# Attention plus two expert layers: value products four head pairs behind the scores, expert 0 released a pair later, and a third PSUM buffer for its first products

## The chip, the cores and the metric

The kernel runs on one core of one Trainium2 chip. The metric is the time of one execution on the device, in microseconds (us). Before the change three executions took 942.99, 941.4 and 942.53 us; the median is 942.53 us. The profile is of a further execution.

The core has five instruction queues that run side by side: TensorE (PE, matrix products into PSUM), VectorE (DVE), ScalarE (ACT), GpSimd (POOL) and SyncE (SP), which here only issues DMAs. Each takes its instructions in the order in which they stand in its queue, so an instruction that waits holds up all that stand behind it.

## The reference

```python
scores = scale * q @ k.T                      # (4, 8, 576, 576), head width 64
scores = where(0 <= rel < 128, scores + alibi, -1e9)
attn   = softmax(scores);  x = attn @ v       # -> x: 2304 tokens x 512
p   = domain_probs / sum(domain_probs)        # 4 experts, dense
out = sum_e p[:, e] * (relu(x @ w1[e]) @ w2[e])          # w1 512x1024, w2 1024x512
logits = out @ phi                            # 8 experts x 4 slots
slots  = softmax(logits, tokens).T @ out      # 32 x 512
slots  = relu(slots @ m1[e]) @ m2[e]          # per expert
return softmax(logits, slots) @ slots         # 2304 x 512
```

## The kernel before, in words

The 2304 tokens are 18 tiles of 128. To keep precision with 16-bit products, nearly every operand is split into a high and a low fp16 half, and a product is three matmuls (high by high, high by low, low by high).

**Attention** goes by head pairs: a tile has 8 heads, so 4 pairs, and the program has 72 of them, numbered 0 to 71 (tile i holds pairs 4i to 4i+3). One pass of the main loop (`for n in range(NS + LAG + 3)`) writes out, in this order:

- `qk` for pair n: the scores, 8 matmuls (12 or 10 where a tile holds the end of a sequence, 4 where it begins one), into one of two PSUM tiles tagged S0 and S1 (lines 336 to 341);
- `soft` for pair n: bias and row minimum on DVE (L353), the exponential on ACT (L358), the high half on ACT (L363), the low half on POOL (L364), and then a transpose of the 128 x 1024 result into `eT`. For tiles 0 and 1 the transposes are done by PE (L303), for the other 16 tiles by a DMA that SP issues (L299);
- the loads and transposes of q, k and v of the next tiles (lines 276 to 321), which use the same SP queue;
- some work of expert 0 from the list `pend`;
- `pv`: the value products of the pair m with `pvt(m) == n` (L381, 12 matmuls). `pvt(m)` is m + 1 for the first four pairs and m + LAG, with LAG = 3, for the rest.

When a tile's last pair has its value products, `xn` and `xn_c` normalise it, split it and transpose it into `xT` (lines 387 to 395 and L299 again).

**Expert 0** works on attention's output as it comes, so that PE has something to do while the chain of DVE, ACT, POOL and SP makes the next `eT`. Tiles are taken in groups: tiles 0 to 3 singly, then by twos. A group becomes available a number of passes after its last value product (`avail`). Its first-layer products are 8 pieces of 12 matmuls (`l1_piece`, L206; called L1.k below, 8 per group, numbered through), 128 columns wide for a single tile and 256 for two. Each piece fills a PSUM tile tagged L1, of which there are two, and is split by ACT (L220) and DVE (L221), which frees the tile. The second layer is 24 matmuls per tile (`l2_mm`, L234) into one of two PSUM tiles tagged L2, and is read by DVE (L242). The tag L2 also serves the PE transposes. A group's second layer is queued between the first-layer pieces of the next group (`queue_moe0`).

The program is recorded with the tile framework, which is asked to schedule it (`schedule_with_timeline_sim=True`): the order of the instructions in each queue is worked out when the kernel is built, with the program's order as priority. So work written later can stand earlier in a queue where its inputs and its buffer are free by then.

After attention come what is left of expert 0, then experts 1 to 3, most of them by seven products in place of eight (L585 and L660), then the slot layer with the loads of `m1` and `m2`.

Of the kernel before, what the change touches and what calls it, by code (L numbers as in the profile page):

```python
# [8 lines left out]
F32 = mybir.dt.float32  # L9
F16 = mybir.dt.float16  # L10
# [9 lines left out]
def kernel(  # L20
# [14 lines left out]
    P = 128  # L35
# [24 lines left out]
    ps = ctx.enter_context(tc.tile_pool(name="ps", bufs=2, space=bass.MemoryType.PSUM))  # L60
    ps2 = ctx.enter_context(tc.tile_pool(name="ps2", bufs=2, space=bass.MemoryType.PSUM))
# [4 lines left out]
    def nm(s):  # L66
        uid[0] += 1
        return f"{s}_{uid[0]}"

    def sl(shape, dt, name, pool=None):  # L70
        return (pool or slab).tile(shape, dt, tag="slab", name=nm(name))
# [101 lines left out]
    def w1_ap(e, fc, hl, kc):  # L173
        o = kc * 256 + (fc % 2) * P
        return W[e, fc // 2, 0][:, hl, o:o + P]
# [12 lines left out]
    def x_ap(t0, n, xa, kc):  # L188
        o = (t0 % TS) * P
        return xT[t0 // TS][:, xa, kc, o:o + n]  # L190
# [8 lines left out]
    hh = {}  # L199

    def l1_piece(e, t0, n, fc, key):
        pt = ps.tile([P, 512], F32, tag="L1", name=nm("l1"))[:, 0:n]
        first_mm = True
        for kc in range(KC):
            for wa, xa in ((0, 0), (0, 1), (1, 0)):
                nc.tensor.matmul(pt, lhsT=w1_ap(e, fc, wa, kc), rhs=x_ap(t0, n, xa, kc),  # L206
                                 start=first_mm, stop=(kc == KC - 1 and wa == 1))
                first_mm = False
        if e == 0:
            kk = (key, fc // 4)  # L210
            if kk not in hh:
                hh[kk] = sl([P, 4, 2, 256], F16, "h")
            ht = hh[kk][:, fc % 4, :, 0:n]
        else:
            kk = (key, fc // 2)
            if kk not in hh:
                hh[kk] = h3[h3n[0] % 2].rearrange("p (a b c) -> p a b c", a=2, b=2)
                h3n[0] += 1
            ht = hh[kk][:, fc % 2, :, 0:n]
        nc.scalar.activation(out=ht[:, 0], in_=pt, func=AF.Relu)  # L220
        nc.vector.scalar_tensor_tensor(out=ht[:, 1], in0=pt, scalar=0.0, in1=ht[:, 0],  # L221
                                       op0=ALU.max, op1=ALU.subtract)

    l2p = {}
    h3n = [0]

    def l2_mm(e, t, o, fcs, key, lo, hi):
# [18 lines left out]
    def moe_pieces(e, tl, fcs, init):  # L246
        key = nm("hk")
        n = len(tl) * P
        r = [(12 * n * 0.422, lambda fc=fc: l1_piece(e, tl[0], n, fc, key)) for fc in fcs]
        for j, t in enumerate(tl):  # L250
            nf = len(fcs)
            for lo in range(0, nf, 4):
                hi = min(lo + 4, nf)

                def f(t=t, j=j, lo=lo, hi=hi):
                    l2_mm(e, t, j * P, fcs, key, lo, hi)
                    if hi == nf:
                        l2_add(e, t, l2p.pop((key, t)), init)
                r.append((3 * (hi - lo) * 216, f))
        return r  # L260
# [5 lines left out]
    sums, nmx, es, eT, xps, xfs = {}, {}, {}, {}, {}, {}  # L266

    def at(shape, dt, tag, bufs=2):
        return ap_.tile(shape, dt, tag=tag, name=nm(tag), bufs=bufs)
# [22 lines left out]
    def sp_v_lo(i):  # L292
        a, t = raw["v", i], vvs[i]
        nc.vector.scalar_tensor_tensor(out=t[:, :, 1], in0=a, scalar=VS, in1=t[:, :, 0],
                                       op0=ALU.mult, op1=ALU.subtract)

    def trans(dst, src, nb, pe):
        if not pe:
            nc.sync.dma_start_transpose(out=dst, in_=src)  # L299
            return  # L300
        pt = ps2.tile([P, 8, P], F16, tag="L2", name=nm("tp"))
        for j in range(nb):
            nc.tensor.transpose(pt[:, j], src[:, j * P:(j + 1) * P], ident16)  # L303
        hb = nb // 2
        nc.vector.tensor_copy(dst[:, 0:hb], pt[:, 0:hb])
        nc.scalar.activation(out=dst[:, hb:nb], in_=pt[:, hb:nb], func=AF.Copy)
# [16 lines left out]
    def kbs(i):  # L323
        return [1] if i in first else [0, 1]
# [19 lines left out]
    def soft(i, hp, st):  # L344
        kb0 = kbs(i)[0]
        if hp == 0:
            sums[i] = at([P, H], F32, "sums")
            nmx[i] = at([P, H], F32, "nmx")
        c0, w = kb0 * P, (2 - kb0) * P
        et = at([P, 2, 2 * P], F32, "e", 3)  # L350
        for hl in range(2):
            h = 2 * hp + hl
            nc.vector.tensor_tensor_reduce(out=et[:, hl, c0:], in0=st[:, hl, c0:], in1=bias[:, h, c0:],  # L353
                                           op0=ALU.add, op1=ALU.min, scale=-0.125, scalar=3.0e38,
                                           accum_out=nmx[i][:, h:h + 1])
        for hl in range(2):
            h = 2 * hp + hl
            nc.scalar.activation(out=et[:, hl, c0:], in_=et[:, hl, c0:], func=AF.Exp, scale=-1.0,  # L358
                                 bias=nmx[i][:, h:h + 1], accum_out=sums[i][:, h:h + 1])
        e2 = at([P, 2, 2, 2 * P], F16, "e2", 3)  # L360
        if kb0:
            e2 = e2.rearrange("p a b c -> p (a b c)")[:, 0:4 * P].rearrange("p (a b c) -> p a b c", a=2, b=2)
        nc.scalar.activation(out=e2[:, :, 0], in_=et[:, :, c0:], func=AF.Copy)  # L363
        nc.gpsimd.tensor_tensor(out=e2[:, :, 1], in0=et[:, :, c0:], in1=e2[:, :, 0], op=ALU.subtract)  # L364
        nb = 4 * w // P
        eTt = at([P, 8, P], F16, "eT", 6)
        trans(eTt[:, 0:nb], e2.rearrange("p a b c -> p (a b c)"), nb, i < 2)
        eT[i, hp] = eTt

# [31 lines left out]

    ld(0)
    bias = at([P, H, 2 * P], BF16, "bias", 1)
    scr = at([P, 2 * P], F32, "scr", 1)
    make_identity(nc, ident16)
    build_bias(scr)
    build_small()
# [14 lines left out]
    swap_q(0)  # L422
    sp_v_hi(0)
    sp_v_lo(0)
    LAG = 3
    NS = NT * 4
    PE_T = 2

    def pvt(m):
        return m + (1 if m < 4 else LAG)  # L430

# [3 lines left out]
        groups0.append(list(range(b0, b0 + z)))  # L435
    avail = []
    for tl in groups0:
        avail.append((pvt(4 * tl[-1] + 3) + (3 if tl[-1] else 1), tl))
    pend = []
    late = []  # L440

# [12 lines left out]
    budget = 0.0  # L454
    for n in range(NS + LAG + 3):
        i, hp = divmod(n, 4)
# [6 lines left out]
        if n < NS:  # L463
            soft(i, hp, st)
# [26 lines left out]
        while avail and avail[0][0] <= n:  # L491
            tl = avail.pop(0)[1]
# [173 lines left out]
    while avail:  # L666
        tl = avail.pop(0)[1]
# [317 lines left out]
    for st in range(2):  # L985
        for hf in range(2):
            hps = ps.tile([P, 512], F32, tag="L1", name=nm("hp"))
            for kc in range(KC):
                for g in range(4):
                    e = 4 * st + g  # L990
# [14 lines left out]
        for g in range(4):  # L1005
            e = 4 * st + g
# [52 lines left out]
```

## Time and profile before

| what | before |
|---|---|
| median of three executions | 942.53 us |
| profiled execution: its time | 942.66 us |
| profiled execution: its span in the profile | 940.9 us |
| PE busy in the span | 877.4 us (93%) |
| DVE, ACT, POOL busy | 577.1, 372.6, 189.3 us |
| mean granted share of PE's clock | 0.983 |

The span is the stretch from the first to the last instruction that the profile shows; the execution's own time lies 1.76 us above it. In the rows below a window `A:B` is in us from the start of the span. `PEclk` is the share of TensorE's full clock of 2.4 GHz that was granted (1.00, or 0.50 at 1.2 GHz; in between it is a mean over the window). A row of the timeline gives start, length, engine, line, operation and tiles; in brackets stands how long the engine was idle just before and what ended it.

### The profile page before, as it was taken

How to read it: one execution, taken by the hardware profiler on the slowest of the kernel's cores; microseconds unless marked ns; L12 is line 12 of the kernel's file. 1: busy time of each engine (PE TensorE's matmuls, PEld its weight loads, DVE VectorE, ACT ScalarE, POOL GpSimd, SP SyncE). 2: the span in 40 equal slices, each digit the busy share in tenths (PEclk: the TensorE clock that was granted, in tenths of full speed). 3: DMA queues.
4: the chain of work that ended last, by engine and by line, in shares of the span. 5: the costliest groups of instructions: out<-in, count | busy, mean ns of one | idle time of the engine just before them, and what ended most of it. 6: DMA issues, size and time to landing. Idle time of an engine off the chain costs nothing.

```text
span 940.9 us, 16481 instructions
## 1 busy us (share of the span) xinstructions
PE 877.4 (93%) x6514; PEld 512.3 (54%) x6514; DVE 577.1 (61%) x1234; ACT 372.6 (40%) x920; POOL 189.3 (20%) x176
## 2 busy tenths in 40 slices
PE   3489988889999999999999999999999999999797
PEld 2366766667765655555555555555555445554432
DVE  9954655576549387657575766666666464456512
ACT  5786666677734243323132323232333202223412
POOL 7765455566420000000000000000000005310000
PEclk9799999999999999999999999999999999999799
DMA  9599999999850110100101010101001008974695
GB/s 261 113 188 183 176 187 154 192 181 186 140 130 28 47 45 3 43 23 22 45 1 45 1 46 1 45 13 33 23 23 46 1 1 326 209 204 139 236 387 222
DMA packets 222031, 102.37 MB, mean 109 GB/s; under 512 B 187217, under 2 KB 201585, under 8 KB 221953
## 3 DMA queue, kind: packets, MB, share of 16 engines
q1 hardware_dynamic: 212320, 78.14, 39.2%
q10 hardware_dynamic: 6800, 13.11, 4.0%
q0 software_dynamic: 2832, 10.07, 2.9%
q8 instruction: 51, 0.84, 0.4%
q14 instruction: 28, 0.22, 0.1%
HBM read 64.59 MB, written 4.72 MB: 74 GB/s over the span
## 4 chain that ended last, share of the span: by engine, by line
PE 76%; DMA 7%; issue 5%; ACT 4%; POOL 3%; DVE 3%; SPq 2%; POOLq 0%; ACTq 0%; DVEq 0%
PE l L660 22%; PE A L585 12%; PE l L206 11%; PE l L234 10%; PE C L585 6%; PE B L585 3%; ACT e L358 2%; PE hp L991 2%; DMA qT<-qs 2%; PE x L381 2%; PE so_ps L1009 2%; DMA m<-in_moe_w_dram 1%; PE s L341 1%; DMA eT<-e 1%; PE fp L1022 1%
## 5 line engine op out<-in xcount | busy, mean ns | idle before, releaser
L660 PE MATMUL l<-w,h 128*128 128x512 f16 x1080 | 252.8, 379 | 0.0
L244 DVE SCALAR_TENSOR_TENSOR acc<-l,pr,acc 128x512 f32<-128x512 f32 x216 | 161.4, 748 | 127.1 <-PE l L660 103.3
L585 PEld LDWEIGHTS <-w 128*128 128x128 f16 x1260 | 123.3, 98 | 94.0
L206 PE MATMUL l<-xT,w 128*128 128x256 f16 (+2 forms) x1344 | 160.5, 271 | 12.6 <-DVE h L221 8.1
L660 PEld LDWEIGHTS <-h 128*128 128x128 f16 x1080 | 105.7, 98 | 115.2
L234 PE MATMUL l<-w,h 128*128 128x512 f16 x648 | 153.1, 381 | 0.7 <-DVE acc L244 0.7
L206 PEld LDWEIGHTS <-w 128*128 128x128 f16 x1344 | 115.9, 99 | 46.2 <-issue 10.1
L609 ACT ACTIVATE ct<-A 128x384 f32<-128x384 f32 x90 | 43.5, 487 | 218.9 <-PE A L585 218.9
L754 POOL DMA_DIRECT2D m<-in_moe_w_dram x19 | 13.8, 725 | 510.1 <-DVE h L605 446.9
L234 PEld LDWEIGHTS <-h 128*128 128x128 f16 x648 | 61.9, 98 | 64.4 <-issue 2.6
L364 POOL TENSOR_TENSOR e<-e,e 128x512 f16<-128x512 f32 (+1 forms) x72 | 81.4, 1133 | 55.7 <-ACT e L363 33.7
L221 DVE SCALAR_TENSOR_TENSOR h<-l,h 128x256 f16<-128x256 f32 (+2 forms) x112 | 45.0, 409 | 62.5 <-ACT h L220 62.1
L220 ACT ACTIVATE h<-l 128x256 f16<-128x256 f32 (+2 forms) x112 | 40.2, 365 | 106.5 <-PE l L206 69.3
L358 ACT ACTIVATE e<-e,nmx 128x256 f32<-128x256 f32 (+1 forms) x144 | 69.9, 487 | 29.3 <-DVE nmx L353 29.1
L585 PE MATMUL C<-xs,w 128*128 128x384 f16 x360 | 71.2, 326 | 0.0
L585 PE MATMUL A<-xs,w 128*128 128x384 f16 x360 | 69.3, 326 | 0.0
L585 PE MATMUL A<-xT,w 128*128 128x384 f16 x360 | 67.6, 326 | 0.0
L353 DVE CUSTOM_DVE_ANT_0 e<-s,bias 128x256 f32<-128x256 f32 (+1 forms) x144 | 52.6, 403 | 19.4 <-PE s L341 15.8
L604 ACT ACTIVATE h<-ct 128x384 f16<-128x384 f32 x90 | 43.8, 515 | 46.5 <-PE l L660 25.1
L336 PE MATMUL s<-kT,qT 128*128 128x128 f16 x272 | 44.9, 228 | 9.3 <-DVE nmx L353 5.1
L381 PE MATMUL x<-vv,eT 128*128 128x64 f16 x816 | 39.3, 197 | 11.5 <-DMA eT<-e 7.3
L605 DVE SCALAR_TENSOR_TENSOR h<-ct,h 128x384 f16<-128x384 f32 x90 | 47.6, 550 | 2.3 <-ACT h L604 2.1
(181 smaller groups left out, 964.6 us busy)
## 6 DMA issues: line engine op xcount, KB each, us to landing
m<-in_moe_w_dram ACTq DMA_DIRECT2D x25, 512.0 KB, 5.5
stg<-in_moe_w_dram SPq DMA_DIRECT2D x20, 512.0 KB, 4.7
m<-in_moe_w_dram SPq DMA_DIRECT2D x20, 512.0 KB, 10.2
m<-in_moe_w_dram POOLq DMA_DIRECT2D x19, 512.0 KB, 11.6
stg<-in_moe_w_dram SPq DMA_DIRECT2D x24, 256.0 KB, 3.3
out_dram<-ots SPq DMA_DIRECT2D x18, 256.0 KB, 3.4
qr<-in_q_dram SPq DMA_DIRECT2D x16, 256.0 KB, 3.8
kr<-in_k_dram SPq DMA_DIRECT2D x16, 256.0 KB, 4.1
```

The source lines that it names most:

```text
L206: nc.tensor.matmul(pt, lhsT=w1_ap(e, fc, wa, kc), rhs=x_ap(t0, n, xa, kc), start=first_mm, stop=(kc == KC - 1 and wa == 1))
L221: nc.vector.scalar_tensor_tensor(out=ht[:, 1], in0=pt, scalar=0.0, in1=ht[:, 0], op0=ALU.max, op1=ALU.subtract)
L234: nc.tensor.matmul(pt, lhsT=ht[:, ha, o:o + P], rhs=w2_ap(e, fc, wa), start=(fc == fcs[0] and ha == 0 and wa == 0), stop=(fc == fcs[-1] an ...
L244: nc.vector.scalar_tensor_tensor(out=a, in0=pt, scalar=p, in1=a, op0=ALU.mult, op1=ALU.add)
L336: nc.tensor.matmul(o, lhsT=qT[i][:, 0, h], rhs=mv, start=True, stop=False)
L353: nc.vector.tensor_tensor_reduce(out=et[:, hl, c0:], in0=st[:, hl, c0:], in1=bias[:, h, c0:], op0=ALU.add, op1=ALU.min, scale=-0.125, scal ...
L358: nc.scalar.activation(out=et[:, hl, c0:], in_=et[:, hl, c0:], func=AF.Exp, scale=-1.0, bias=nmx[i][:, h:h + 1], accum_out=sums[i][:, h:h ...
L364: nc.gpsimd.tensor_tensor(out=e2[:, :, 1], in0=et[:, :, c0:], in1=e2[:, :, 0], op=ALU.subtract)
L381: nc.tensor.matmul(o, lhsT=t[:, (hl * 2 + ea) * nk + kb - kb0], rhs=vvs[i - 1 + kb][:, h, va], start=(kb == kb0 and ea == 0 and va == 0), ...
L585: nc.tensor.matmul(o, lhsT=wq_[:, blk, wa, kc], rhs=xf(xa, kc), start=(first and kc == 0 and wa == 0 and xa == 0), stop=(kc == 1 and wa == 1),
L605: nc.vector.scalar_tensor_tensor(out=o[:, 1], in0=src, scalar=0.0, in1=o[:, 0], op0=ALU.max, op1=ALU.subtract)
L660: nc.tensor.matmul(pt, lhsT=u["h"][:, z, ha, par, i * P:(i + 1) * P], rhs=w2_ap(e, 2 * qd + z, wa), start=(z == 0 and ha == 0 and wa == 0) ...
```

## The change

The value products trail the scores by four pairs (LAG = 4). The release of a group of expert 0 is counted from the value products, so it moves along; for groups that end at tile 2 or later it is one pair later still. Every third first-layer piece of expert 0 takes its PSUM tile from the tag L2 in place of L1. `eT` has seven buffers for six, and the scratch tile of the bias borrows the first of `e`'s three buffers, which makes the room.

```diff
     def l1_piece(e, t0, n, fc, key):
-        pt = ps.tile([P, 512], F32, tag="L1", name=nm("l1"))[:, 0:n]
+        l1n[0] += e == 0
+        pool, tg = (ps2, "L2") if e == 0 and l1n[0] % 3 == 0 else (ps, "L1")
+        pt = pool.tile([P, 512], F32, tag=tg, name=nm("l1"))[:, 0:n]
...
     l2p = {}
+    l1n = [0]
...
-        eTt = at([P, 8, P], F16, "eT", 6)
+        eTt = at([P, 8, P], F16, "eT", 7)
...
-    scr = at([P, 2 * P], F32, "scr", 1)
+    scr = at([P, 2, 2 * P], F32, "e", 3)[:, 0]
...
-    LAG = 3
+    LAG = 4
...
-        avail.append((pvt(4 * tl[-1] + 3) + (3 if tl[-1] else 1), tl))
+        avail.append((pvt(4 * tl[-1] + 3) + (4 if tl[-1] > 1 else 3 if tl[-1] else 1), tl))
```

The number of instructions on every engine stays the same; the schedule gives them another order up to the end of expert 0, and nearly the same one after it. Three places are shown. The changed kernel's line numbers are 3 higher from its second edit on (2 higher inside `l1_piece`), and the numbers in tile names are given anew.

SP's queue, where the DMA transposes of `eT` begin (pair 8). `qT` and `kT` are the transposed q and k of tiles 3 and 4, `qr`, `kr`, `vr` loads; `eT_703` and `eT_740` are pairs 8 and 9. Before:

```order
L299 DMA_TRANSPOSE qT_745<-qs_708 128x8x128
L299 DMA_TRANSPOSE kT_784<-ks_747 128x8x128
L276 DMA qr_875<-in_q_dram 128x8x64
L276 DMA kr_911<-in_k_dram 128x8x64
L276 DMA vr_1023<-in_v_dram 128x8x64
L299 DMA_TRANSPOSE eT_703<-e_117_700 128x8x128
L299 DMA_TRANSPOSE qT_913<-qs_877 128x8x128
L299 DMA_TRANSPOSE eT_740<-e_123_737 128x8x128
L299 DMA_TRANSPOSE kT_1025<-ks_915 128x8x128
```

Now, with `eT_690` and `eT_728` as pairs 8 and 9:

```order
L302 DMA_TRANSPOSE qT_733<-qs_695 128x8x128
L302 DMA_TRANSPOSE kT_772<-ks_735 128x8x128
L279 DMA qr_862<-in_q_dram 128x8x64
L279 DMA kr_899<-in_k_dram 128x8x64
L279 DMA vr_937<-in_v_dram 128x8x64
L302 DMA_TRANSPOSE qT_901<-qs_864 128x8x128
L302 DMA_TRANSPOSE kT_939<-ks_903 128x8x128
L302 DMA_TRANSPOSE eT_690<-e_116_687 128x8x128
L302 DMA_TRANSPOSE eT_728<-e_123_725 128x8x128
```

Both transposes of tile 4 now stand ahead of those of pairs 8 and 9.

PE's queue from the scores of pair 28 to the first product of tiles 4 and 5 (L1.32), one row for each step. Before, `s_1951`, `s_1989` and `s_2089` are the scores of pairs 28 to 30, `eT_1806` the value products of pair 25, `l_330_2116` a second layer, `l_318_2016` L1.32:

```order
L336 MATMUL s_1951<-kT_1600,qT_1810 128x128
...
L381 MATMUL x_1938<-vv_1347,eT_1806 128x64
...
L234 MATMUL l_330_2116<-w_312,h_1562 128x512
...
L336 MATMUL s_1989<-kT_1600,qT_1810 128x128
...
L336 MATMUL s_2089<-kT_1600,qT_1810 128x128
...
L206 MATMUL l_318_2016<-xT_445,w_206 128x256
```

Now, `s_1929`, `s_1977`, `s_2015`, `s_2054` and `s_2148` are pairs 28 to 32, `eT_1709`, `eT_1763` and `eT_1832` the value products of pairs 24 to 26, `l_329_2075` L1.32:

```order
L339 MATMUL s_1929<-kT_1572,qT_1767 128x128
...
L384 MATMUL x_1964<-vv_1260,eT_1709 128x64
...
L384 MATMUL x_1964<-vv_1260,eT_1763 128x64
...
L339 MATMUL s_1977<-kT_1572,qT_1767 128x128
...
L384 MATMUL x_1964<-vv_1260,eT_1832 128x64
...
L339 MATMUL s_2015<-kT_1572,qT_1767 128x128
...
L339 MATMUL s_2054<-kT_1572,qT_1767 128x128
...
L339 MATMUL s_2148<-kT_1836,qT_1998 128x128
...
L208 MATMUL l_329_2075<-xT_445,w_206 128x256
```

The second-layer products (19 matmuls in a row before) have left this stretch; they stand behind L1.35 now, and two more pairs' scores stand ahead of L1.32.

PE's queue around the value products of pair 42, one row for each step. Before, `s_2903` and `s_2959` are the scores of pairs 45 and 46, `eT_2763` is pair 42, `l_466_2931` is L1.48, the first product of tiles 8 and 9:

```order
L381 MATMUL x_2838<-vv_2359,eT_2703 128x64
...
L336 MATMUL s_2903<-kT_2545,qT_2707 128x128
...
L381 MATMUL x_2838<-vv_2359,eT_2763 128x64
...
L336 MATMUL s_2959<-kT_2545,qT_2707 128x128
...
L206 MATMUL l_466_2931<-xT_2168,w_206 128x256
```

Now, with `s_2917` and `s_2970` as pairs 46 and 47, `eT_2713` as pair 42 and `l_477_2991` as L1.48:

```order
L384 MATMUL x_2835<-vv_2289,eT_2668 128x64
...
L339 MATMUL s_2917<-kT_2488,qT_2672 128x128
...
L237 MATMUL l_442_2780<-w_394,h_2249 128x512
...
L384 MATMUL x_2835<-vv_2289,eT_2713 128x64
...
L339 MATMUL s_2970<-kT_2488,qT_2672 128x128
...
L208 MATMUL l_477_2991<-xT_2177,w_206 128x256
```

Pair 42's value products now stand behind the scores of pair 46 and 12 second-layer matmuls; L1.48 stands one pair later.

## Rows read from the trace of the kernel before

**Rows 1.** The page: busy time of each engine, share of the span, instructions.

```profile
PE 877.4 (93%) x6514; PEld 512.3 (54%) x6514; DVE 577.1 (61%) x1234; ACT 372.6 (40%) x920; POOL 189.3 (20%) x176
```

**Rows 2.** Windows: length; busy PE, PEld, DVE, ACT, POOL; PEclk; DMA share; GB/s.

```profile
45.00:65.00 20.00, 15.40 (x247) 12.75 (x244) 12.98 (x47) 16.07 (x50) 13.59 (x12) 1.00 0.97 174
65.00:114.00 49.00, 45.26 (x614) 33.89 (x612) 25.64 (x90) 31.43 (x95) 25.91 (x22) 0.97 1.14 192
114.00:124.00 10.00, 8.53 (x105) 6.06 (x102) 7.97 (x28) 8.20 (x26) 6.78 (x6) 1.00 0.95 136
124.00:157.00 33.00, 28.16 (x311) 20.67 (x310) 15.28 (x54) 20.38 (x62) 17.61 (x17) 1.00 1.05 183
157.00:245.00 88.00, 80.02 (x905) 60.09 (x904) 56.89 (x172) 62.90 (x180) 51.44 (x44) 0.96 1.04 177
245.00:275.00 30.00, 30.00 (x331) 21.78 (x328) 13.94 (x49) 15.99 (x47) 12.68 (x11) 1.00 0.63 107
275.00:800.00 525.00, 525.00 (x2862) 279.89 (x2861) 338.80 (x567) 150.00 (x310) 15.36 (x21) 1.00 0.13 42
```

**Rows 3.** What PE waited for from 45 to 275: us in total, times, longest.

```profile
PE l L206 <- DVE h L221: 8.1, 6, 2.4
PE x L381 <- DMA eT<-e: 7.3, 6, 2.4
PE l L206 <- DMA xT<-xs: 3.5, 2, 2.0
PE s L336 <- DVE nmx L353: 2.6, 1, 2.6
```

**Rows 4.** Timeline of PE at five of its waits.

```profile
93.94 0.83 PE L206 MATMUL l<-xT,w 128*128 128x128 f16 x12 [2.24 <-DVE h L221]
...
123.35 2.79 PE L206 MATMUL l<-xT,w 128*128 128x256 f16 x24 [1.47 <-DMA xT<-xs]
...
151.72 0.52 PE L381 MATMUL x<-vv,eT 128*128 128x64 f16 x12 [2.43 <-DMA eT<-e]
...
178.04 0.52 PE L381 MATMUL x<-vv,eT 128*128 128x64 f16 x12 [1.85 <-DMA eT<-e]
...
180.69 2.52 PE L206 MATMUL l<-xT,w 128*128 128x256 f16 x12 [2.02 <-DMA xT<-xs]
```

**Rows 5.** Windows around the three stretches at half clock, and one wait without.

```profile
91.00:95.00 4.00, 1.76 (x39) 1.49 (x35) 1.92 (x7) 1.50 (x6) 2.15 (x2) 1.00 1.02 197
95.00:100.00 5.00, 5.00 (x57) 3.95 (x55) 2.60 (x12) 3.60 (x12) 1.15 (x1) 0.66 0.97 195
138.00:142.00 4.00, 1.59 (x21) 1.38 (x19) 2.38 (x9) 2.72 (x8) 1.15 (x1) 1.00 1.01 209
177.00:181.00 4.00, 0.94 (x17) 0.75 (x18) 1.62 (x2) 2.05 (x4) 3.08 (x3) 1.00 1.00 200
181.00:185.00 4.00, 4.00 (x22) 2.63 (x21) 2.88 (x11) 2.53 (x9) 1.04 (x2) 0.58 1.21 228
...
198.00:202.00 4.00, 4.00 (x32) 2.77 (x30) 2.91 (x11) 3.97 (x14) 1.89 (x2) 0.57 0.90 175
```

**Rows 6.** The chain that ended last, from 244 to 262: start, us, what.

```profile
254.45 0.35 PE x L381 x12
...
255.25 0.35 PE x L381 x12
...
256.04 2.62 PE l L206 x24
```

**Rows 7.** SP's queue, line 299: ns min/median/max, first and last start.

```profile
L299 SPq DMA_TRANSPOSE eT<-e x64: 1205/1291/2581, 53.3 to 267.2; - x64
```

**Rows 8.** Timeline of SP where the transposes of eT begin.

```profile
55.34 1.25 SPq L299 DMA_TRANSPOSE qT<-qs  x1
...
58.08 1.51 SPq L299 DMA_TRANSPOSE kT<-ks  x1
```

**Rows 9.** Timeline of PE: the value products of pair 23.

```profile
113.44 0.51 PE L381 MATMUL x<-vv,eT 128*128 128x64 f16 x12
```

## The prediction, made before the changed kernel was run

> **What bounds the kernel now.** I read the page first: PE is busy for 93% of the span, no other engine for more than 61% [rows 1]. Then busy time by stretch, which shows where PE's idle time lies [rows 2]. From 245 to 800 PE is busy without a gap, so nothing there can be gained but by taking work out, and the change takes none out: every engine has as many instructions as before, and the order after expert 0 is nearly the same. Up to 45 the first loads and the first tiles rule, and the order there is the same as well. What is left is 45 to 245. In the five windows that cover it PE is idle for 4.60, 3.74, 1.47, 4.84 and 7.98 us, together 22.6 (length less busy PE) [rows 2]. The list of waits says for what: 8.1 us for DVE to empty a PSUM tile of the first layer, 7.3 for the DMA that brings `eT`, 3.5 for the DMA that brings `xT`, 2.6 for DVE to empty a score tile [rows 3]; the rest is the start. The timeline gives the single waits, none over 2.63 us [rows 3, 4].
>
> To that comes the clock. Three stretches ran at 1.2 GHz: the windows at 95, 181 and 198 have a granted clock of 0.66, 0.58 and 0.57 with PE busy throughout, which is 0.34 x 5 + 0.42 x 4 + 0.43 x 4 = 5.1 us lost. Before the first two PE had been busy for 1.76 and 0.94 of 4 us [rows 5]. So 22.6 + 5.1 = 27.7 us are the whole of what this change can give back, 2.9% of the time.
>
> The rest of PE's time up to the end of attention is work that stays. At full clock a pair's value products take 0.35 us and its scores 0.45 (255.25 less 254.45 less 0.35), two 256-column pieces of the first layer 2.62 [rows 6]. A piece of expert 0 that is not done during attention is done after it at the same cost, with PE busy. What counts is therefore only how much idle time and how much half clock there is in the new order; I go through it by the five stretches.
>
> **45 to 65 (pairs 8 to 16).** SP's queue has the transposes of tile 4's q and k ahead of that of pair 8. They took 1.25 and 1.51 us [rows 8], so pair 8's `eT` comes up to 2.8 us later, and POOL must make those halves first. The value products of pairs 8 to 10 stand close together on PE with little else between them, since the pieces L1.0 to L1.7 are all queued ahead. Bounds: no loss, if the low half of pair 8 is late anyway, and 2.8 us. I take two thirds of it: idle 4.6 + 1.8 = 6.4.
>
> **65 to 114.** 3.74 us of idle, all before first-layer products that waited for DVE; 2.24 of it at 93.94 [rows 2, 4]. With three PSUM tiles in rotation such a piece waits for the split three pieces back and not two; a 128-column piece is some 0.8 us [rows 4], so the third tile covers one such step and the later lag and release put other work there too. Bounds 0 and 3.74; I take 0.5. What is late next is PE's own work.
>
> **114 to 124 (pairs 27 to 32).** Here the order gets worse. The second layer that ran between the scores of pairs 28 and 29 has moved behind L1.35, since L1.32 and L1.35 take L2 tiles ahead of it. From the end of pair 23's value products, which open tiles 4 and 5, to L1.32 it took 123.35 - 113.95 = 9.4 us, and L1.32 waited 1.47 of them for `xT` [rows 4, 9]. That path (normalise, split, SP, DMA) is not shortened. PE now has between the two only the scores of five pairs and the value products of three: 5 x 0.45 + 3 x 0.35 = 3.3. Idle: 9.4 - 3.3 = 6.1, for 1.47 now. Bounds: 1.47, if the scores spread over the same time as now, and above by the pace of the chain: SP's seven transposes per tile at 1.29 us [rows 7] are 2.26 us a pair, five pairs 11.3, less 3.3, is 8.0. I take 6.1.
>
> **124 to 157 (pairs 33 to 43).** The wait of 2.4 us for DVE before a first-layer piece [rows 3] goes, that of 2.43 before pair 34's value products [rows 4] goes with the longer lag. But L1.40 again needs the last value products of its group, pair 31, and behind them stand only the scores of pairs 36 to 42, the first four of them half as long (4 x 0.22 + 3 x 0.45 = 2.2), and the value products of four pairs (1.4). By the same 9.4 us the idle time is 5.8, for 4.84 now. Bounds 2.4 (one wait as now), and by SP's pace 7 x 2.26 - 3.6 = 12.2.
>
> **157 to 245 (pairs 44 to 63).** The order is even here: with each pair come its scores, the value products of the pair four back and one or two pieces of expert 0. The waits of 1.85 (`eT`) and 2.02 (`xT`) at 178 to 181 [rows 4] go: pair 42's products stand a pair and 12 second-layer matmuls later, and L1.48 behind them. The wait for DVE of 2.63 [rows 3] came from a score tile and may stay in part. Bounds 0 and 7.98; I take 1.5.
>
> The other two edits cost nothing: `scr` is read by DVE before the first scores, long before its buffer is wanted again, and a seventh `eT` buffer holds the one pair more that is now under way.
>
> **The clock.** All three present stretches at half clock follow waits that I let go. In the new order PE is thinly busy in the two bare stretches (3.3 of 9.4 us and 3.6 of 9.4), about as thinly as before two of the present three, while after 138 to 142 with 1.59 of 4 us busy it did not fall [rows 5]. I take one stretch of 1.7 us for each of the two, 3.4 for 5.1. Bounds 0 and 8.5 (one in each of the five stretches).
>
> The Trainium skill speaks against the change here: "TensorE: Matmul & The Clock Gate", section "Part 1: The HAM clock gate", has the low clock as the state that an engine falls back to and activity as what lifts it. By that rule the thin stretch at 45 to 65 would cost a third fall, and the sum would be 1.7 us higher. The trace agrees in the three falls and not in the wait at 138.
>
> **The sum.** Idle 6.4 + 0.5 + 6.1 + 5.8 + 1.5 = 20.3 for 22.6, half clock 3.4 for 5.1: 4.0 us less. The profiled execution took 942.66 us, of which 940.9 are its span; 942.66 - 4.0 = 938.7. The median shown is 942.53, 0.13 below the profiled one; I let that stand and predict 938.7.
>
> **Rivals.**
>
> *The bare stretches are paced by the chain (slower).* A score tile is free for the pair after next only when DVE has read it, and DVE, ACT and POOL go on only as their buffers come free behind SP's transposes. If pairs 28 to 32 and 36 to 42 go at SP's 2.26 us a pair, the two stretches cost 8.0 + 12.2 and not 11.9, and the stretch before each gives a third fall of the clock: 938.7 + 8.3 + 1.7 = 948.7. It decides from 4 us more idle time than I put there, about 16 us in the two together. For it: `eT` transposes now start 213.9 us apart over 63 steps, 3.4 us a pair, and the new order starves this chain while PE does expert 0 in long blocks. Against it: the buffers let two or three pairs of scores run ahead, and the path to `xT` ends first. Chance 0.21.
>
> *The waits stay where the lag does not reach.* From 157 on only the waits for `eT` go (1.85 and what is like it), while those for `xT` and for DVE (2.02 + 2.63 = 4.65) stay in some form: 938.7 + 4.65 - 1.5 = 941.8. For it: the change does nothing to the path from value products to `xT`. A form of it is that the third PSUM tile does not help, as two of three pieces still share two tiles: 65 to 114 keeps 3.74 us and its fall of the clock, 938.7 + 3.2 + 1.7 = 943.6. Chance of both together 0.24; both are no change.
>
> *The bare stretches cost nothing.* If value products and scores spread so that PE idles there no longer than now (1.47 + 4.84 = 6.3 for 11.9) and the clock holds, 938.7 - 5.6 - 3.4 = 929.7. Chance 0.08.
>
> **How the numbers follow.** My forecast has 0.47, with a range of its own of 934 to 941. About 0.2% (1.9 us) is what a measurement of this kernel can tell from no change, since its three executions lie 1.6 us apart; the forecast and the last rival are faster by more, the second lies within, the first is slower. Some of the forecast's spread falls within 0.2%, some of the middle rival's outside it on either side: 0.54 faster, 0.24 the same, 0.22 slower. For 8 in 10 the range leaves out the last rival and the outer half of the first: 931.5 to 947.
>
> **What would show it.** Right: from 65 to 114 and from 157 to 245 PE is idle for under 3 us in all, no wait for `eT` behind pair 40; an idle stretch of 5 to 7 us ends with L1.32 on `xT`, a second with L1.40; attention's last value products come 5 to 9 us earlier than now. Wrong: L1.32 starts later than about 125 us or L1.40 later than about 155 (the chain sets the pace), falls of the clock at more than two places, or waits of 2 us and more among pairs 44 to 63. If PE idles anywhere between 245 and 800, the order behind attention matters after all, and the sum lacks a term.

## The result, and the profile after

| what | before | after |
|---|---|---|
| median | 942.18 us (6 runs, 941.09 to 945.7) | 950.05 us (6 runs, 947.66 to 952.67) |
| ratio | | 1.0077, 95% interval 1.006 to 1.0093 |
| profiled execution: time, span | 942.66, 940.9 us | 947.66, 945.9 us |
| mean granted share of PE's clock | 0.983 | 0.979 |

The change makes the kernel 0.8% slower. The forecast was 938.7 us with a range of 931.5 to 947: the time lies above the range, and the sign is wrong too. The execution that was profiled is the fastest of the six after; the other five had a mean clock of 0.966 to 0.973. Part of that distance is no difference in time: the profiled execution has no record of the clock before 51.94 us, and time without a record counts as full clock.

The first row of the page of the profile after, beside [rows 1]: as many instructions, and PE busy for 9.2 us more.

```profile
PE 886.6 (94%) x6514; PEld 521.3 (55%) x6514; DVE 579.5 (61%) x1234; ACT 370.8 (39%) x920; POOL 191.2 (20%) x176
```

PE did not get more work; it did part of it at half the clock. The windows of the kernel after, in the stretches and columns of [rows 2]:

```profile
45.00:65.00 20.00, 16.08 (x234) 15.29 (x232) 13.44 (x47) 15.55 (x47) 11.93 (x11) 0.93 1.02 161
65.00:114.00 49.00, 47.54 (x599) 35.78 (x597) 28.02 (x88) 30.52 (x94) 26.36 (x23) 0.92 1.04 178
114.00:124.00 10.00, 7.71 (x123) 5.77 (x122) 7.22 (x24) 6.82 (x23) 5.19 (x5) 1.00 1.06 189
124.00:157.00 33.00, 25.77 (x284) 19.85 (x285) 20.09 (x61) 22.47 (x69) 20.13 (x17) 0.86 1.05 185
157.00:245.00 88.00, 83.92 (x871) 60.59 (x870) 50.07 (x168) 57.56 (x170) 51.15 (x44) 0.96 1.03 170
245.00:275.00 30.00, 29.10 (x339) 21.52 (x337) 14.79 (x48) 18.25 (x54) 14.00 (x12) 1.00 0.80 137
275.00:800.00 525.00, 525.00 (x2886) 281.39 (x2885) 337.34 (x566) 149.01 (x308) 12.76 (x18) 1.00 0.11 37
```

Idle time (length less busy PE) is 3.92 + 1.46 + 2.29 + 7.23 + 4.08 + 0.90 = 19.9 us from 45 to 275, for 22.6 before. So PE idles 2.75 us less. But PEclk is 0.93, 0.92 and 0.86 where it had been 1.00, 0.97 and 1.00. The single stretches at half clock, in a view of windows with the same columns, then the stretch behind them, and at the end the start of expert 0:

```profile
62.18:65.60 3.42, 3.22 (x47) 3.07 (x48) 2.06 (x9) 3.25 (x9) 3.16 (x4) 0.50 1.02 212
69.01:75.84 6.83, 6.83 (x59) 5.68 (x59) 3.17 (x9) 3.23 (x9) 3.42 (x3) 0.50 1.18 180
127.04:133.86 6.82, 5.16 (x25) 3.57 (x25) 1.96 (x6) 2.11 (x6) 3.50 (x4) 0.50 1.10 169
154.34:164.58 10.24, 7.04 (x44) 5.24 (x43) 9.40 (x28) 7.64 (x26) 7.86 (x8) 0.50 0.78 154
164.60:245.00 80.40, 77.67 (x836) 56.17 (x834) 43.29 (x146) 51.55 (x151) 45.07 (x38) 1.00 1.06 173
45.00:52.00 7.00, 5.82 (x60) 5.71 (x57) 4.39 (x14) 4.59 (x15) 2.81 (x3) 1.00 0.86 109
```

At half clock half of the busy time is lost (the matmuls of a pair's scores start 0.107 us apart at 157.9 us and 0.054 at 125.5): (3.22 + 6.83 + 5.16 + 7.04) / 2 = 11.1 us, for 5.1 before. The four stretches lie in or just behind pairs 13 to 18, 27 to 32 and 36 to 42, where scores follow scores with hardly a product of expert 0 between. From 164.6 to 275 the clock is full.

Ahead of three of the falls PE had idled: 2.48 us up to 62.34, and in the first two rows below. Ahead of the fall at 69.0 it had not; it ran scores and other short matmuls for 3.34 of 3.41 us (third row):

```profile
118.37:127.04 8.67, 3.96 (x77) 3.24 (x74) 5.98 (x22) 7.05 (x21) 4.85 (x5) 1.00 1.03 204
150.11:154.34 4.23, 2.93 (x65) 2.33 (x62) 4.18 (x13) 4.12 (x14) 3.05 (x3) 1.00 0.76 146
65.60:69.01 3.41, 3.34 (x32) 1.95 (x30) 1.89 (x9) 2.59 (x10) 2.23 (x2) 1.00 1.23 231
```

The last row of the windows further up, 45:52, is a trap: its PEclk says 1.00, since the clock's records begin at 51.94 in this execution. The durations of the matmuls tell otherwise. The group of line 208 (206 before) from 46 to 56 us, ns min/median/max of one; first after:

```profile
L208 PE MATMUL l<-xT,w x72: 219/298/314, 46.6 to 54.7; 128*128 128x128 f16 x72
```

The same in the kernel before:

```profile
L206 PE MATMUL l<-xT,w x60: 216/219/219, 46.7 to 55.5; 128*128 128x128 f16 x60
```

So after the change PE came up to full clock at about 51.9 us; before, the record of half clock ends at 44.4. By estimate that costs 5.82 / 2 = 2.9 us more.

What PE waited for from 45 to 275, beside [rows 3]: the waits for the split of a first-layer result (`h`) have fallen from 8.1 to 0.4 us, and those for `eT` from 7.3 to 5.0. In their place PE waits for DVE to read a score tile (`nmx`, 7.5 us for 2.6) and for `xT` (5.6 for 3.5).

```profile
PE s L339 <- DVE nmx L356: 7.5, 8, 1.8
PE l L208 <- DMA xT<-xs: 5.6, 4, 2.6
PE x L384 <- DMA eT<-e: 5.0, 5, 2.5
PE l L208 <- DVE xT L308: 1.2, 1, 1.2
PE l L208 <- DVE h L223: 0.4, 1, 0.4
```

### The profile page after: what moved, and what is told of

It reads as the page before. It is cut to its first block, busy times and chain, and to the rows that moved or that the text cites. A ratio compares the mean times of both kernels' runs of the same rounds, so it can differ in the third digit from the quotient of the medians.

```text
span 945.9 us, 16469 instructions
## 1 busy us (share of the span) xinstructions
PE 886.6 (94%) x6514; PEld 521.3 (55%) x6514; DVE 579.5 (61%) x1234; ACT 370.8 (39%) x920; POOL 191.2 (20%) x176
## 4 chain that ended last, share of the span: by engine, by line
PE 76%; DMA 9%; issue 5%; DVE 5%; POOL 2%; SPq 2%; ACT 1%; POOLq 0%; ACTq 0%; DVEq 0%
PE l L663 22%; PE A L588 12%; PE l L208 11%; PE l L237 10%; PE C L588 6%; PE B L588 3%; DMA eT<-e 2%; DMA qT<-qs 2%; PE hp L994 2%; DMA xT<-xs 2%; DMA kT<-ks 2%; PE so_ps L1012 1%; PE x L384 1%; DMA m<-in_moe_w_dram 1%; PE fp L1025 1%
## 5 line engine op out<-in xcount | busy, mean ns | idle before, releaser
L588 PEld LDWEIGHTS <-w 128*128 128x128 f16 x1260 | 123.2, 98 | 93.3
L208 PE MATMUL l<-xT,w 128*128 128x256 f16 (+2 forms) x1344 | 164.3, 279 | 7.2 <-DMA xT<-xs 5.6
L208 PEld LDWEIGHTS <-w 128*128 128x128 f16 x1344 | 121.2, 103 | 41.2 <-issue 5.9
L607 ACT ACTIVATE h<-ct 128x384 f16<-128x384 f32 x90 | 44.2, 515 | 44.4 <-PE l L663 27.0
L339 PE MATMUL s<-kT,qT 128*128 128x128 f16 x272 | 46.7, 236 | 14.1 <-DVE nmx L356 10.0
L615 DVE TENSOR_TENSOR ct<-ct,C 128x384 f32<-128x384 f32 x60 | 33.0, 550 | 29.1 <-ACT ct L612 18.9
## 6 DMA issues: line engine op xcount, KB each, us to landing
m<-in_moe_w_dram SPq DMA_DIRECT2D x20, 512.0 KB, 10.2
```

What stands on the lines that cost most here:

```text
L339: nc.tensor.matmul(o, lhsT=qT[i][:, 0, h], rhs=mv, start=True, stop=False)
L588: nc.tensor.matmul(o, lhsT=wq_[:, blk, wa, kc], rhs=xf(xa, kc), start=(first and kc == 0 and wa == 0 and xa == 0), stop=(kc == 1 and wa == 1),
L607: nc.scalar.activation(out=o[:, 0], in_=src, func=AF.Relu)
```

## The experiments

Each is the kernel before or after with the edit shown. "Idle" and "lost" are of PE from 60 to 170 us in the profiled execution, a stretch that leaves the start of expert 0 out: idle is 110 less busy PE, lost is half of PE's busy time within the stretches at half clock. "Bare" counts the pairs behind pair 9 whose scores stand in PE's order in runs of three or more without a product of expert 0 between; rows of fewer than six such products are not counted as one. Behind 170 the kernels differ too: there the kernel before idles 7.9 us and loses 3.4 to the clock, the changed one 3.6 and 0.

| kernel | bare pairs | idle | lost | median, us | ratio to before, 95% |
|---|---|---|---|---|---|
| before | 0 | 11.7 | 1.7 | 942.2 | |
| after | 22 | 14.7 | 11.1 | 950.05 | 1.0077 (1.006 to 1.0093) |
| third buffer only | 19 | 17.5 | 8.2 | 947.1 | 1.0046 (1.0033 to 1.006) |
| lag and release | 3 | 14.1 | 0.0 | 940.11 | 0.997 (0.9957 to 0.9983) |
| lag only | 6 | 10.0 | 3.4 | 939.87 | 0.9971 (0.9956 to 0.9985) |
| release only | 0 | 10.8 | 1.7 | 942.62 | 0.999 (0.997 to 1.001) |
| after, 38 matmuls in bare pairs | 20 | 10.6 | 4.3 | 949.3 | 1.0063 (1.0041 to 1.0085) |
| after, 76 matmuls in bare pairs | 21 | 8.7 | 3.1 | 951.84 | 1.0095 (1.0076 to 1.0113) |
| after, 38 matmuls in dense pairs | 22 | 13.6 | 16.0 | 957.33 | 1.0157 (1.0124 to 1.0191) |
| lag, third buffer for piece 7 | 0 | 11.2 | 1.7 | 936.74 | 0.9942 (0.9922 to 0.9962) |
| after, third buffer for piece 7 | 4 | 12.1 | 3.0 | 941.34 | 0.9982 (0.9962 to 1.0002) |
| third buffer for piece 7 only | 3 | 12.9 | 3.2 | 943.11 | 0.9989 (0.9969 to 1.001) |
| lag and third buffer | 21 | 14.1 | 10.1 | 949.62 | 1.0066 (1.0045 to 1.0086) |

The median of before was 942.5 to 942.9 in the three sets of experiments.

**My theory** (theory A in the expectations). A tile of a tag is handed out in the program's order. A first-layer piece of a new group that takes an L2 tile stands in the program ahead of second-layer work of the old group, and it waits for the new group's `xT`. So the second layer, which is ready, can't be scheduled ahead of it; PE is left with scores alone, goes thin, and the clock falls. The second place in the section on the change shows the order: the second layer has left the scores of pairs 28 and 29 and stands behind L1.35. **Rivals:** the longer lag or the later release costs (the chain behind the scores paces the bare pairs), rival B of the first four runs; or the falls of the clock are chance, rival C.

### The parts of the change

Third buffer only:

```diff
+        l1n[0] += e == 0
+        pool, tg = (ps2, "L2") if e == 0 and l1n[0] % 3 == 0 else (ps, "L1")
```

> Only the third PSUM buffer is kept (every third first-layer piece of expert 0 takes an L2 tile); lag and release are as before. Its order has three stretches of 6, 7 and 6 pairs of scores with no expert 0 in between (pairs 13-18, 26-32, 34-39). Theory A (the L2 tiles taken by first-layer pieces bar the second layer from filling in, and PE's clock falls in the bare stretches): slower than before by 4 to 10 us, 20 us or more of the stretch 45 to 275 at half clock, idle time about as before (20 to 24 us). Rival B (the later value products and the later release starve PE of expert 0's work, the third buffer helps): 2 to 8 us faster than before, since 8.1 us of waits for DVE go. Rival C (the falls of the clock are chance of the run): within 2 us of before, and falls at other places than those stretches.

Lag and release, without the third buffer (the seventh `eT` buffer and the borrowed scratch tile go with the lag):

```diff
-    LAG = 3
+    LAG = 4
...
-        avail.append((pvt(4 * tl[-1] + 3) + (3 if tl[-1] else 1), tl))
+        avail.append((pvt(4 * tl[-1] + 3) + (4 if tl[-1] > 1 else 3 if tl[-1] else 1), tl))
```

> The change without the third PSUM buffer: lag of four pairs, later release, seven eT buffers. Its order has no bare stretch of more than 3 pairs behind pair 9. Theory A: no slower than before, 0 to 5 us faster, at most 10 us of 45 to 275 at half clock, and the waits for eT mostly gone while those for DVE (8.1 us before) stay. Rival B: slower by 4 to 8 us, with idle time over 26 us from 45 to 275. Rival C: like the changed kernel, 3 to 10 us slower, as its clock falls by chance too.

Lag only (with its buffers), and release only, each with its line of the diff above:

> Only the lag of four pairs (with the seventh eT buffer and the borrowed scratch it needs); release counted as before, two L1 tiles. Theory A: within 3 us of before, waits for eT (7.3 us before) under 3 us, half clock at most 10 us. Rival B: if the lag itself is what costs, 3 to 7 us slower; if only the extra release costs, as before.

> Only the release one pair later for groups that end at tile 2 or behind it. Theory A: within 3 us of before (the wait of L1.32 and L1.48 for xT, 3.5 us, goes in part), no new bare stretch, half clock at most 10 us. Rival B: 3 us or more slower, since PE runs out of expert 0's work earlier.

Measured: the third buffer alone makes the kernel slower (ratio 1.0046), lag and release without it faster (0.997), the lag alone just as much, the release alone changes nothing that can be told. Both rivals fall: the lag is a gain, and the two kernels with the third buffer lose 8 to 11 us to the clock between 60 and 170, the four without it 0 to 3.4. That is one profile of each; the mean clock of every execution speaks against chance as well. Its median is 0.967 in the changed kernel, 0.9765 with the third buffer alone and 0.975 in the kernel with lag and third buffer below. It is 0.980 or more in the kernel before (57 executions), in the three others without the third buffer, and in the three below that take it for piece 7. The window of the third buffer alone, from 60 to 170 (PE busy first, PEclk third from the end):

```profile
60.00:170.00 110.00, 92.52 (x1100) 69.57 (x1101) 62.74 (x196) 70.20 (x208) 58.77 (x52) 0.91 0.99 172
```

And of lag and release without it:

```profile
60.00:170.00 110.00, 95.92 (x1231) 72.90 (x1229) 62.50 (x220) 75.30 (x228) 65.92 (x57) 1.00 1.09 187
```

PE is idle for 17.5 and 14.1 us; the second kernel's clock did not fall there at all, though it idles more than the kernel before (11.7). How long PE idles in sum does not settle whether the clock falls.

One expectation failed: with the lag the waits for `eT` were to go for the most part, and they did not. From 45 to 275, lag and release first, then the lag alone (7.3 us before):

```profile
PE x L381 <- DMA eT<-e: 7.1, 9, 1.3
PE x L381 <- DMA eT<-e: 5.3, 5, 1.3
```

So what the lag gains is not shown to come from these waits.

### Does the order of the pieces do it?

The change without the later release, and with the L2 tile for another piece:

```diff
-        pool, tg = (ps2, "L2") if e == 0 and l1n[0] % 3 == 0 else (ps, "L1")
+        pool, tg = (ps2, "L2") if e == 0 and fc == 7 else (ps, "L1")
```

Piece 7 is the last of its group. When it is written, the L2 tiles for the second layer of the group before have all been handed out.

> The lag of four with its buffers, without the later release; the tile tagged L2 is taken for the last of the eight first-layer pieces of a group in place of every third piece. The last piece stands behind the second layer of the group before, so that it does not hold this back: in PE's order no scores of three or more pairs follow one another without a product of expert 0 between. Theory A (what the third buffer costs in the change is that its place in the order bares the scores): no more half clock than with the lag alone (5.1 us lost) and a little less waiting for the split of a first-layer result (7.3 us with the lag alone): 936 to 940.5 us. Rival B (sharing the tag L2 is what costs, by the PE transposes or the second layer waiting for a tile): 942 to 948 us.

Measured: 936.74 us, the fastest kernel of this study and faster than both that were given. Windows from 60 to 170 and behind:

```profile
60.00:170.00 110.00, 98.81 (x1253) 75.77 (x1254) 70.15 (x221) 76.48 (x232) 64.93 (x57) 0.98 1.06 185
170.00:275.00 105.00, 101.77 (x1102) 73.26 (x1101) 60.78 (x190) 67.36 (x194) 56.17 (x48) 1.00 0.97 172
```

The clock fell once between 60 and 275, at 107.4, and the waits for `h` are 5.8 us from 45 to 275 (7.3 with the lag alone):

```profile
PE l L208 <- DVE h L223: 5.8, 4, 3.1
PE s L339 <- DVE nmx L356: 4.3, 3, 2.1
```

The whole change with the same one-line edit, the piece alone on the kernel before, and the change without the later release:

> The whole change with one difference: the tile tagged L2 is taken for the last of the eight first-layer pieces of a group in place of every third piece. In PE's order one stretch of four pairs (38 to 41) is left without a product of expert 0 between the scores; the changed kernel has four such stretches with 22 pairs. Theory A (which pieces take the tile decides, since a piece that stands ahead of the second layer in the program holds it back): 936 to 942 us, a fall of 8 to 14 us from the changed kernel, with 3.4 to 5.1 us lost at half clock between 45 and 275 for 11.1. Rival D (the later release does not go with the third buffer): 945 us or more.

> The kernel before, with the third buffer alone, taken for the last piece of a group. PE's order has one stretch of three pairs (44 to 46) without a product of expert 0. Theory A: 938.5 to 942.5 us, the waits for the split of a first-layer result below the 8.1 us of before, half clock as before (5.1 us lost). Rival B (a third tile for the first layer costs in itself): 945 to 948 us, as the third buffer at every third piece (947.1).

> The change without the later release: lag of four and every third piece in a tile tagged L2. In PE's order pairs 13 to 18, 19 to 21, 27 to 32 and 35 to 40 have no product of expert 0 between, 21 pairs against 22 in the change. The third buffer alone cost 4.6 us, the lag alone gained 2.6 and the whole change lost 7.9: the parts do not add up. Theory A (the bare stretches decide, and the lag adds the one at 19 to 21 and moves another): 947 to 952 us, 9 to 13 us lost at half clock between 45 and 275. Rival D (what the whole loses beyond its parts comes with the later release): 943.5 to 946 us.

Measured: 941.34, 943.11 and 949.62 us. The first is the sharpest test: it differs from the changed kernel in nothing but which pieces take the L2 tile, and it is 8.7 us faster, with the intervals of the two ratios far apart. Its windows, and then the changed kernel's from 45 to 275:

```profile
60.00:170.00 110.00, 97.87 (x1224) 74.10 (x1225) 66.90 (x218) 75.81 (x229) 64.63 (x57) 0.97 1.06 179
45.00:275.00 230.00, 209.36 (x2491) 157.72 (x2489) 132.75 (x437) 153.77 (x456) 127.16 (x111) 0.97 1.02 171
...
45.00:275.00 230.00, 210.11 (x2442) 158.80 (x2440) 133.62 (x434) 151.18 (x453) 128.76 (x110) 0.94 1.01 170
```

Against the changed kernel idle fell by 2.6 us and lost clock by 8.1 between 60 and 170. From 45 to 275 the two idle about alike, 20.6 and 19.9 us, so the difference of the two profiled executions, 941.10 and 947.66, is left to the clock: 6.2 us lost there (3.2 of them at the start, where its record of half clock ends at 52.5) against 11.1 and the 2.9 at the start. That 6.2 is above the 3.4 to 5.1 that I expected.

The third fits theory A: without the later release the loss stays. The lag's gain is gone there: 949.62 is no faster than the 947.1 of the third buffer alone (the intervals overlap). Two expectations of the second missed: the waits for `h` did not fall below 8.1 us, they were 10.0; and the median, 943.11, was 0.6 above what I expected, but can't be told from the kernel before. So at piece 7 the third buffer alone gains nothing that can be told. The later release costs in one of two comparisons: with lag and piece 7 it is 941.34 with it and 936.74 without, the intervals touching at 0.9962; with the lag and no third buffer 940.11 and 939.87. Why, I did not follow up.

### Does the clock cost the time?

The changed kernel with matmuls added in the bare pairs, before the scores that overwrite them:

```diff
+        if 4 * i + hp in WARM:
+            for z in range(2):
+                nc.tensor.matmul(st.rearrange("p a b -> p (a b)"), lhsT=qT[i][:, 0, 2 * hp], rhs=kT[i][:, 0:4].rearrange("p h t -> p (h t)"),
+                                 start=True, stop=True)
```

> The changed kernel with work added: ahead of the scores of pairs 13 to 18, 27 to 32 and 36 to 42 (19 pairs, those whose scores follow one another with no product of expert 0 between) two matmuls of 512 columns each are written into the score tile and overwritten by the scores. They use the same operands as the scores. 38 x 0.216 = 8.2 us of PE work at full clock, of which perhaps 6 fits into PE's idle time there (10.4 us in the stretches 45 to 65, 114 to 124 and 124 to 157 of the profile after, by estimate). Theory A (the change loses by the clock: 11.1 us lost at half clock between 45 and 275, all but 1 us of it at or just after these pairs): the stretches at half clock at 62, 69, 127 and 154 go or shrink to under half, and the time falls from 950.0 although PE does more: 942 to 947 us. Rival B (the bare pairs lose by the chain from DVE to the transposes, and the clock falls are no cause of the time): 951 to 956 us. Rival C (the stretches at half clock fall by chance): the time falls or rises without the falls sitting elsewhere than before.

The same with four for two, and with the two in dense pairs:

> As the run before with four matmuls of 512 columns for two, 76 x 0.216 = 16.4 us of PE work at full clock. Theory A: no stretch at half clock is left between 60 and 170 us; the time is that of the changed kernel less some 10 us of clock, plus what of the 16.4 does not fit into idle time, some 6 to 10 us: 945 to 951 us. Rival B: 956 to 962 us.

> Control for the price of the added matmuls: the changed kernel with the same 38 matmuls ahead of the scores of pairs 46 to 64, where products of expert 0 stand between the scores and no stretch ran at half clock except at most one. Theory A and rival B alike: the falls at 62, 69, 127 and 154 stay, and the time rises by 8.2 us less what fits into idle time there (4.1 us between 157 and 245): 954 to 958 us.

Measured: 949.3, 951.84 and 957.33 us. The same 38 matmuls cost 7.3 us over the changed kernel in dense pairs and nothing that can be told in the bare ones (949.3 for 950.05). The windows of the kernel with 38 in bare pairs, at the places where the changed kernel's clock had fallen:

```profile
62.07:65.49 3.42, 2.82 (x32) 2.12 (x33) 2.28 (x8) 2.87 (x8) 2.44 (x3) 0.50 0.99 203
69.00:76.00 7.00, 6.47 (x78) 4.68 (x77) 2.60 (x9) 3.74 (x11) 2.29 (x3) 1.00 1.25 177
126.93:133.75 6.82, 5.72 (x30) 3.94 (x31) 2.59 (x13) 4.37 (x13) 4.86 (x5) 0.50 1.17 209
154.30:164.60 10.30, 9.14 (x84) 6.66 (x85) 8.62 (x24) 9.03 (x30) 8.72 (x9) 1.00 0.85 175
```

The falls at 69 and 154 are gone, those at 62 and 127 stayed; from 60 to 170 lost clock went from 11.1 to 4.3 us and idle from 14.7 to 10.6. Together that is 10.9 us back for 8.2 of work. In all four executions the mean clock is 0.978 to 0.988, with a median of 0.986 for the changed kernel's 0.967. The time did not fall to the 942 to 947 that theory A gave. One reason is in its timeline: ahead of the fall at 127 PE stood idle for longer than in the changed kernel, before an added matmul.

```profile
128.03 1.01 PE L338 MATMUL s<-kT,qT 128*128 128x512 f16 x2 [3.55 <-issue]
```

Another: the profile has a further fall from 208.9 to 215.7. So work in the bare pairs lifts the clock in part, and theory A's number was too low. With 76 matmuls its expectations missed too: two falls of 3.4 us were left between 60 and 170, at 62.9 and 155.1, where none was to be, and 951.84 lies above its 945 to 951. The control's profiled execution was its slowest (961.98) and ran at half clock from 61.2 to 78.3; its lost 16.0 is not that of its median. Up to there its order is the changed kernel's, so how long the clock stays low differs between executions of the same order.

## Why the prediction was wrong

**What bounds the kernel: right, but for the start.** From the end of attention's last value products to the end of the span the two profiles take 669.0 and 669.8 us; nothing there needs a term of its own. PE idled for 0.90 us between 245 and 275 where it had none. The start did need a term: it was put at nothing, since the order up to 45 is the same, and full clock came 7.5 us later.

**Idle time in sum: right, in part by luck.** Forecast was 20.3 for 22.6, measured 19.9. The stretches miss by 0.9 to 3.8 us on either side and cancel, and work at half clock fills time that would be idle. By stretch:

- *45 to 65* was put at 6.4 and came to 3.92.
- *65 to 114* was put at 0.5 and came to 1.46; the waits for `h` went, as forecast.
- *The bare pairs* came out near the forecast, only later, so that 114 to 124 has 2.29 us of idle time and 124 to 157 7.23. The timeline of PE at pairs 27 to 32:

```profile
119.52 0.52 PE L384 MATMUL x<-vv,eT 128*128 128x64 f16 x12 [0.70 <-DMA eT<-e]
120.89 0.52 PE L384 MATMUL x<-vv,eT 128*128 128x64 f16 x12 [0.85 <-DMA eT<-e]
...
122.23 0.52 PE L384 MATMUL x<-vv,eT 128*128 128x64 f16 x12 [0.37 <-DMA eT<-e]
...
125.46 0.22 PE L339 MATMUL s<-kT,qT 128*128 128x128 f16 x1 [1.81 <-DVE nmx L356]
...
128.70 7.47 PE L208 MATMUL l<-xT,w 128*128 128x256 f16 x44 [2.63 <-DMA xT<-xs]
```

The five gaps add up to 6.36 us (forecast 6.1), and the last ends on `xT` with L1.32, as forecast. Waits for `eT` and for a score tile are among them, which the prediction did not name for this stretch. From the end of pair 23's value products to L1.32 it took 10.33 us (9.4 by [rows 4, 9]), and from the end of pair 31's to L1.40 10.48. Windows of the two:

```profile
118.37:128.70 10.33, 3.97 (x78) 3.24 (x75) 5.98 (x22) 7.74 (x23) 6.51 (x6) 0.92 1.06 180
150.11:160.59 10.48, 5.99 (x89) 4.71 (x86) 9.72 (x29) 9.36 (x29) 8.15 (x8) 0.70 0.86 169
```

- The second has 4.49 us idle, for 5.8. Of its 5.99 us of busy PE 3.06 ran at half clock; at full clock the idle time would be 6.0, by estimate.
- *157 to 245* was put at 1.5 and came to 4.08, part of it still of the second bare stretch; from 164.6 to 245 it is 2.73. No wait for `eT` is left behind pair 40.

**The clock: this step failed.** It read: "I take one stretch of 1.7 us for each of the two, 3.4 for 5.1. Bounds 0 and 8.5". The stretches measured 11.1 us, above the upper bound. Two things were wrong. I priced a fall at the length of the three in [rows 5], 3.4 us; three of the four that came were 6.8, 6.8 and 10.2 us long, the last with PE busy for 7.04 of them. The trace before holds a row that shows a longer one, ahead of expert 0, with PE busy for 4.43 of 10.2 us:

```profile
34.20:44.40 10.20, 4.43 (x44) 3.41 (x44) 9.48 (x19) 7.99 (x20) 8.35 (x7) 0.50 0.43 85
```

And I put no fall into 45 to 65, which I had costed as idle time alone, and did not see that pairs 13 to 18 stand bare; there came two falls, at 62.2 and 69.0, for 5.0 us. The prediction's own sign of being wrong, falls at more than two places, came; its sign of being right, under 3 us idle in 65 to 114 and 157 to 245 together, did not (5.54). The Trainium skill, in "TensorE: Matmul & The Clock Gate", section "Part 1: The HAM clock gate", has the low clock as the state that the engine falls back to when activity is missing. The trace after agrees in the fall at 62.2, behind a wait of 2.48 us, and less plainly in the one at 69.0, ahead of which PE was busy for 3.34 of 3.41 us. I had set the rule aside for this stretch on the wait at 138 that brought no fall; the two cost three times the 1.7 us that I gave for it.

**The sum again, with measured terms:** 942.66 - 2.75 (idle) + 6.0 (clock, 11.1 for 5.1) + 2.9 (the late rise at the start) = 948.8; the profiled execution took 947.66. 1.15 us too much, which I did not trace. The median lies 2.4 us above the profiled execution, and none of the slower five was profiled. Attention's last value products ended at 276.14 for 271.86, where I had forecast 5 to 9 us earlier.

**The rivals.** *Bare stretches paced by the chain* gave 948.7, near the time that was measured, and for another reason: it needed 16 us of idle time in the two, and there were 6.36 + 4.49 = 10.9. Its sign, L1.32 behind 125 and L1.40 behind 155, did come (128.70 and 160.59). It misled: the value products of pair 23 ahead of them ended 4.4 us late already (118.37 for 113.95), behind 2.9 and 5.0 us lost to half clock, for 1.7 before. A sign that is an absolute time adds up all that came before; the length from pair 23's value products to L1.32 would have told the cases apart. *Waits stay* is partly so: those for `xT` and the score tile stayed and grew (5.6 and 7.5 us from 45 to 275). Its form in which the third buffer does not help is refuted, as the waits for `h` went. *Bare stretches cost nothing* is refuted.

**The cause, as far as shown.** That the choice of pieces for the L2 tile makes the loss is shown, by the kernel that changes it alone (8.7 us). That it does so by the clock is read from one profile of each (from 45 to 275 they idle alike) and from the mean clock of all executions, and is borne out in part by the added matmuls. Why some thin stretches bring a fall and others none, why one came behind a stretch that was not idle, and what sets their length stays open.

## What to carry to other kernels

When a buffer's tag is shared, ask in which order the program asks for its tiles: an early taker that must wait holds up every later user, even one that is ready. Price a new order by where PE goes thin, not by idle time in sum: here the two bare stretches that were foreseen idled for 10.9 us, and the falls of the clock in and behind them cost 6.1 more. If one more buffer is wanted, try it for the work that stands last in line; in this kernel that took the loss away, and with the lag alone it made the fastest time.

## What the runs showed of the hardware

- Full clock came between 44.4 and 52.5 us in the profiles that were taken: 44.4 before, 44.4 with the lag alone, 51.9 after. In the four profiles without a third buffer it came by 48.3, in the nine with one from 49.3 on. PE's order is the same in all of them up to about 44.9 us. There it parts: with the third buffer eight transposes, which share the tag L2, stand later. First before, then after:

```profile
44.90 0.61 PE L303 MATMUL tp<-ident,e 128*128 128x128 f16 x8
...
54.73 1.06 PE L306 MATMUL tp<-ident,e 128*128 128x128 f16 x16
```

  Before, full clock came ahead of that place, so the order cannot be the whole of it. Whether the third buffer or chance makes it late stays open.
- The kernel with lag and release but no third buffer, with 14.1 us idle between 60 and 170, kept the full clock there; the one before, with 11.7, did not.
- A window's PEclk reads 1.00 where the execution has no record of the clock yet; the duration of the matmuls (298 ns median for 219) tells the level.
